# One load for the values of a turn, the output products ahead of them, and closing products in four column groups: an attention decode step on one core

## The chip, the core and the metric

The kernel runs on one core of a Trainium2 chip. Time is device time in microseconds (us) of one launch, and the smaller is the better. Before the change three runs gave 220.52, 220.58 and 221.18 us; the median is 220.58 us.

The engines named here are TensorE (PE in the rows; its weight loads are PEld), VectorE (DVE), ScalarE (ACT), GpSimd (POOL) and SyncE (SP, which here only waits and asks for transfers). Sixteen DMA engines carry the transfers; all of this kernel's transfers stand in one queue that SP fills.

## The reference: what is computed

One decode step for a batch of two tokens, in float32. Two branches are mixed by a gate.

```python
g = sigmoid((x * gate_w).sum(-1))                  # x: 2 x 512
q = (x @ wq)                                       # 32 heads of 128
k, v = the last 4096 rows of the caches            # 8 key heads, each shared by 4 query heads
p = softmax(q k^T / sqrt(128));  o = p v
a = o @ wo                                         # wo: 4096 x 512
b = mish(x @ w1 + b1) @ w2                         # 512 -> 1792 -> 512
out = g * a + (1 - g) * b                          # 2 x 512
```

Per key head, K and V of both batches are 4 MB each, wq's and wo's share 1 MB each. Everything that is read is read once, 91.26 MB in all.

## The kernel before, in words

The work goes in eight turns, one for each key head, in a hardware loop on each engine (`Fori(1, HKV + 1)`). SP's part is written out, without a loop. There is one buffer for K with the next turn's wq (`kslot`, 40 KB per partition) and one for V with w2's and wo's share (`vslot`). Semaphores tie the engines together; `ld_...` are counted up by transfers, 16 for each.

In a turn TensorE does the scores (L233), a small transpose for the maximum (L239), the sum of the exponentials (L240), the values (L244), the second product of the dense branch (L253), a selection of the attention output (L257) and the output products with wo (L260). Scores, values, w2 and wo products are 32 columns wide on the output side, so four of them stand in the four column groups of the array and run at the same time. A float32 matmul shows up as two instructions in the rows.

The dense branch and the output products lag by a turn: the `wst` and `hst` that L260 and L253 multiply in turn r were written by GpSimd at the end of turn r-1 (semaphore `hs`), and the wo and w2 that come into `vslot` beside V of turn r are those of turn r-1. They add into `acc`, in PSUM, over all turns. What is left after the eighth turn, wo of the last head, comes in three loads into `wol` and is multiplied by the closing products (L267), which add it up in `fin` with the folded `acc` (through `accs`, ScalarE's copy at L218).

VectorE in a turn makes the next turn's queries (L325, which end in `qz`), the maximum (L329), the transposed probabilities `pT` (L335), the dense branch's first product (L336, L292, L298), scales the attention output (L342, L344, giving `osel`), and copies the selected output into `wst2` (L347, semaphore `wst`).

SP's order for turn i (counted from 0): wait for `qz`, so that the scores are done with `kslot`; ask for K of turn i; wait for `sV`, which TensorE counts up after the first half of the values; ask for the first half of V (`va`); wait for `sP`, which it counts up at the end of the turn, after L260; ask for the second half of V with w2 and wo (`vb`). The last turn's K, V, w2 and wo come in smaller pieces, and the closing wo in three (`wo7a`, `wo7b`, `wo7c`). After that SP waits for `res` and stores the 4 KB result.

At the end, TensorE's closing products write two rows of 256 columns at a time: for u of 0 and 1 into column groups 0 and 1 or 2 and 3. ScalarE copies one half out (L220, `fs`), VectorE adds the other to it (L351).

Of the kernel before, what the change touches and what calls it, by code (L numbers as in the profile page):

```python
# [3 lines left out]
F32 = mybir.dt.float32  # L4
# [4 lines left out]
P = 128  # L9
B = 2  # L10
# [26 lines left out]
def decode_kernel(nc, xg, wq0, w1, kw, k7a, k7b, k7c, va, vb0, vb, v7b, v7c, w26, wo6, wo7a, wo7b, wo7c, out):  # L37
# [5 lines left out]
    def ps(name, n):  # L43
# [6 lines left out]
    vslot = sb("vslot", CHUNK + 2 * D + WQH + 2 * HKV)  # L50
    vs, w2s, wos = vslot[:, :CHUNK], vslot[:, CHUNK : CHUNK + 2 * D], vslot[:, CHUNK + 2 * D : CHUNK + 2 * D + WQH]
    b1 = vslot[:, CHUNK + 2 * D + WQH : CHUNK + 2 * D + WQH + FC]
# [41 lines left out]
    fs = sb("fs", 256, 64)  # L94
    res = sb("res", 256, 64)
# [10 lines left out]
    names = ("ld_x ld_q ld_k ld_kb ld_kc ld_v ld_vb ld_vc ld_w ld_h ld_o ld_w0 ld_w1 ld_w2 c_id c_m c_z c_xb c_eg c_g c_mg "  # L106
             "gx g0 g1 g2 g3 g4 g5 hs vx q8 rcp os1 os2 os3 qz mx sA sB bias ex pT sC osel sD sP sE sV wst pq mkr w1c w1p hx hq hd hr accs pe fs res st").split()
# [3 lines left out]
    SP.dma_start(vslot[:, CHUNK + 2 * D : CHUNK + 2 * D + WQH + FC], wq0).then_inc(sem["ld_q"], L)  # L111
# [4 lines left out]
    for i in range(HKV):  # L116
# [7 lines left out]
        if i:  # L124
            SP.wait_ge(sem["sV"], i)
        SP.dma_start(vs[:, : 2 * h], va[i]).then_inc(sem["ld_v"], L)
        if i:
            SP.wait_ge(sem["sP"], i)
        if i == 0:
            SP.dma_start(vs[:, 2 * h :], vb0).then_inc(sem["ld_vb"], L)  # L130
            SP.dma_start(w1s[:, : PAIRS * W1P], w1).then_inc(sem["ld_w"], L)
        elif i < PAIRS:
            SP.dma_start(vslot[:, 2 * h : CHUNK + 2 * D + WQH], vb[i - 1]).then_inc(sem["ld_vb"], L)
        else:
            SP.dma_start(vs[:, 2 * h : 3 * h], v7b).then_inc(sem["ld_vb"], L)
            SP.dma_start(vs[:, 3 * h :], v7c).then_inc(sem["ld_vc"], L)
            SP.dma_start(w2s, w26).then_inc(sem["ld_h"], L)  # L137
    SP.dma_start(wos, wo6).then_inc(sem["ld_o"], L)
# [69 lines left out]
    for n in ("ld_kb", "ld_kc", "ld_vc", "ld_o", "ld_h"):  # L208
        A.sem_inc(sem[n], AHEAD)
# [9 lines left out]
    A.wait_ge(sem["pe"], 1)  # L219
    A.copy(fs, fin[64:, :256]).then_inc(sem["fs"], 1)  # L220


    key_rhs = same[:, :16].rearrange("p (b n h) -> p b n h", b=B, n=NH)[:, :, 0, :]
    with T.Fori(1, HKV + 1, 1) as r:
# [16 lines left out]
        T.wait_ge(sem["ld_v"], loads)  # L241
        for c in range(NC):
# [162 lines left out]
```

## Time and profile before

| what | value |
|---|---|
| three runs, median | 220.58 us |
| profiled execution, its own time | 220.1 us |
| its span, first to last instruction of the program | 218.8 us |
| moved | 91.26 MB, 417 GB/s over the span |
| mean granted TensorE clock | 0.797 of full |
| TensorE busy / VectorE busy | 118.8 us / 126.2 us |

The profiled execution's time is 1.3 us above its span (220.1 - 218.8) and 0.5 us under the median of the three runs. Its rows read like this: a start and a duration in us from the span's start, engine, line of the kernel, operation, what it writes and reads, how many instructions the row stands for, and in brackets how long the engine was idle before it and what ended that.

### The profile page before, as it was taken

The numbers are of one execution on the slowest core, as the hardware profiler recorded it, in microseconds if no ns is written. First come the engines' busy times: TensorE is split into PE (matmuls) and PEld (weight loads), VectorE is DVE, ScalarE is ACT, GpSimd is POOL, SyncE is SP. The second block draws the span as 40 slices with busy tenths as digits, with TensorE's granted clock in tenths as the row PEclk, the third lists the DMA queues.
The fourth block names the chain that finished last, engine by engine and source line by source line (L and its number), as shares of the span: only waits on it lengthen the run. The fifth ranks groups of instructions, "written<-read, shape, count | busy, mean of one in ns | idle before, by whom it ended". The sixth has DMA issues, their size and how long they took to land.

```text
span 218.8 us, 1985 instructions
## 1 busy us (share of the span) xinstructions
PE 118.8 (54%) x668; PEld 31.1 (14%) x668; DVE 126.2 (58%) x268; ACT 10.3 (5%) x28; POOL 26.2 (12%) x118
## 2 busy tenths in 40 slices
PE   0006386058463477807547195924648175984775
PEld 0002021012110112202111022101112022120211
DVE  2897913919743468507673177714693075967850
ACT  2000010000100001000100001000100001000101
POOL 8200000220021000310012000210002100050030
PEclk9999958757969675875988757695996958599599
DMA  8898999989999999989999899999999899999993
GB/s 310 367 479 371 453 446 407 479 377 429 451 434 442 401 437 455 464 374 452 435 407 479 377 429 446 439 442 401 437 455 464 374 446 440 392 412 442 412 410 118
DMA packets 4926, 91.29 MB, mean 417 GB/s; under 512 B 552, under 2 KB 572, under 8 KB 1084
## 3 DMA queue, kind: packets, MB, share of 16 engines
q1 hardware_dynamic: 4924, 91.26, 97.8%
q8 instruction: 1, 0.02, 0.0%
q14 instruction: 1, 0.01, 0.0%
HBM read 91.26 MB, written 0.00 MB: 417 GB/s over the span
## 4 chain that ended last, share of the span: by engine, by line
DMA 73%; PE 15%; DVE 8%; SPq 2%; issue 1%; DVEq 0%
DMA vslot<-in_vb 51%; DMA w1s<-in_w 15%; PE o L244 9%; DMA wol<-in_wo7a 8%; PE acc L260 4%; DVE osc L344 3%; PE small L257 1%; DVE osc L342 1%; DVE junk L292 1%; DVE hxt L298 1%; PE fin L267 1%; SPq L113 0%; DVE w1c L336 0%; DVE xs L300 0%; SPq L137 0%
## 5 line engine op out<-in xcount | busy, mean ns | idle before, releaser
L233 PE MATMUL sc<-kslot,zeros 128*32 128x512 f32 x256 | 42.7, 823 | 51.5 <-DMA kslot<-in_kw 50.2
L325 DVE CUSTOM_DVE_ANT_0 junk<-kslot,xs 128x512 f32<-128x512 f32 x64 | 39.8, 686 | 37.4 <-DMA kslot<-in_kw 36.4
L244 PE MATMUL o<-vslot,pT 128*32 128x512 f32 x256 | 48.2, 897 | 12.8 <-DMA vslot<-in_vb 10.1
L233 PEld LDWEIGHTS sc<-kslot,zeros 128*32 128x32 f32 x256 | 10.7, 145 | 83.2 <-issue 80.4
L187 POOL TENSOR_TENSOR hb<-hxt,zeros 128x4 f32<-128x4 f32 x8 | 1.7, 216 | 147.0 <-DVE hxt L298 147.0
L292 DVE TENSOR_TENSOR junk<-w1c,xs 128x2048 f32<-128x2048 f32 x8 | 18.3, 2293 | 0.3
L298 DVE TENSOR_REDUCE hxt<-junk 128x4 f32<-128x2048 f32 x8 | 18.3, 2286 | 0.3
L244 PEld LDWEIGHTS o<-vslot,pT 128*32 128x32 f32 x256 | 9.2, 147 | 42.4 <-issue 19.1
L342 DVE TENSOR_SCALAR osc<-o,mkr 128x128 f32<-128x128 f32 x8 | 2.8, 351 | 15.1 <-PE o L244 15.1
L214 ACT ACTIVATE prob<-sc,bias 128x512 f32<-128x512 f32 x8 | 5.5, 687 | 118.7 <-DVE bias L333 118.7
L257 PE MATMUL small<-same,osc 128*128 128x8 f32 x16 | 3.3, 280 | 12.7 <-DVE osc L344 12.7
L240 PE MATMUL small<-lsum,same 128*128 128x1 f32 x16 | 4.1, 324 | 10.5 <-ACT prob L214 10.5
L260 PE MATMUL acc<-vslot,zeros 128*32 128x512 f32 x64 | 9.4, 662 | 0.6 <-DMA vslot<-in_wo 0.6
L335 DVE STREAM_TRANSPOSE pT<-prob 128x512 f32<-128x512 f32 x8 | 5.7, 712 | 6.8 <-ACT prob L214 6.8
L336 DVE COPY w1c<-w1s 128x1024 f32 x8 | 5.2, 656 | 7.5 <-DMA w1s<-in_w 7.5
L344 DVE SCALAR_TENSOR_TENSOR osc<-o,mkr,osc 128x128 f32<-128x128 f32 x24 | 8.4, 351 | 0.9
L253 PE MATMUL acc<-vslot,zeros 128*32 128x512 f32 x32 | 8.6, 616 | 0.3 <-DMA vslot<-in_w 0.3
L329 DVE TENSOR_REDUCE mx<-sc 128x1 f32<-128x512 f32 x8 | 5.5, 691 | 5.6 <-PE sc L233 5.6
L239 PE MATMUL mb<-ident,mx 128*128 128x128 f32 x8 | 2.6, 322 | 9.1 <-DVE mx L329 9.1
L257 PEld LDWEIGHTS small<-same,osc 128*128 128x128 f32 x16 | 2.6, 203 | 20.2 <-DVE osc L344 20.2
L325 DVE DVE_READ_ACCUMULATOR2_ANT q<- 128x1 f32 x64 | 5.2, 81 | 0.0
L240 PEld LDWEIGHTS small<-lsum,same 128*128 128x128 f32 x16 | 3.4, 265 | 12.0 <-ACT prob L214 12.0
(63 smaller groups left out, 64.8 us busy)
## 6 DMA issues: line engine op xcount, KB each, us to landing
kslot<-in_kw SPq DMA_DIRECT2D x7, 5120.0 KB, 19.3
vslot<-in_vb SPq DMA_DIRECT2D x6, 3584.0 KB, 18.9
vslot<-in_va SPq DMA_DIRECT2D x8, 2048.0 KB, 19.9
w1s<-in_w SPq DMA_DIRECT2D x1, 3584.0 KB, 32.7
vslot<-in_vb SPq DMA_DIRECT2D x1, 2048.0 KB, 24.6
kslot<-in_k7a SPq DMA_DIRECT2D x1, 2048.0 KB, 11.1
vslot<-in_wq SPq DMA_DIRECT2D x1, 1031.0 KB, 5.2
kslot<-in_k7b SPq DMA_DIRECT2D x1, 1024.0 KB, 13.2
```

The lines of the kernel that those rows point to most:

```text
L214: A.activation(prob, sc, AF.Exp, bias=bias, scale=SCALE, accum_out=lsum).then_inc(sem["ex"], 1)
L233: i = T.matmul(sc[Q * j : Q * j + Q, :], qz[:, m * Q : m * Q + Q], ks[:, (m * NJ + j) * 512 : (m * NJ + j + 1) * 512], start=(m == 0), sto ...
L240: after(T.matmul(lp, same, lsum, start=True, stop=True), "ex").then_inc(sem["sC"], 1)
L244: i = T.matmul(o[Q * j : Q * j + Q, :], pT[:, c * Q : c * Q + Q], vs[:, c * 512 : c * 512 + 512], start=(c < NJ), stop=(c >= NC - NJ))
L253: i = T.matmul(acc[Q * j : Q * j + Q, :], hst[:, j * Q : j * Q + Q], w2s[:, j * D : j * D + D], start=False, stop=False, skip_group_check= ...
L257: after(T.matmul(ol, osel, key_rhs, start=True, stop=True), "osel").then_inc(sem["sE"], 1)
L260: i = T.matmul(acc[Q * j : Q * j + Q, :], wst[:, j * Q : j * Q + Q], wos[:, j * D : j * D + D], start=False, stop=False, skip_group_check= ...
L292: return V.tensor_tensor(out.rearrange("p (b c d) -> p b c d", b=B, c=n), lhs.rearrange("p (c d) -> p c d", c=n)[:, None, :, :].to_broadca ...
L298: return V.tensor_reduce(out, junk[:, : n * D].rearrange("p (c d) -> p c d", d=D), axis=AX.X, op=ALU.add)
L325: i = V.tensor_tensor_reduce(out=junk[:, (h * B + b) * D : (h * B + b) * D + D], in0=wqs[:, h * D : h * D + D], in1=xb[b], op0=ALU.mult, o ...
L335: after(V.transpose(pT, prob), "ex").then_inc(sem["pT"], 1)
L344: after(V.scalar_tensor_tensor(osc[:, m * DH : m * DH + DH], o[:, m * DH : m * DH + DH], mkr[:, m : m + 1], osc[:, m * DH - DH : m * DH], ...
```

## The change

Three things are changed.

First, V of a turn comes in one load. `vslot` now begins with 64 bytes that hold b1 in the first turn, then wo, V and w2 in this order. Turns 1 to 6 have one load for the whole row (`vw`, 44 KB per partition), turn 0 one for V, and in turn 7 wo's share comes with the first half of V (`v7a`). The semaphore `sV` is gone; SP asks for the whole of V after `sP`.

Second, TensorE's order in a turn: the four wo products stand ahead of the values, the two w2 products behind the values as before, and `sP` is now counted up behind w2, ahead of the selection product. The loop's first instruction is put at an address that is a multiple of 256 (`T.addr_align`).

Third, the closing products. Each of the five operands is multiplied by four matmuls of 128 columns, one in each column group; the folded `acc` comes first; VectorE copies the sum out at once (128 x 128), and ScalarE's copy and the addition are gone. The output is stored from eight rows of 512 bytes.

```diff
-        if i:
-            SP.wait_ge(sem["sV"], i)
-        SP.dma_start(vs[:, : 2 * h], va[i]).then_inc(sem["ld_v"], L)
-        if i:
-            SP.wait_ge(sem["sP"], i)
         if i == 0:
-            SP.dma_start(vs[:, 2 * h :], vb0).then_inc(sem["ld_vb"], L)
+            SP.dma_start(vs, v0).then_inc(sem["ld_v"], L)
             SP.dma_start(w1s[:, : PAIRS * W1P], w1).then_inc(sem["ld_w"], L)
-        elif i < PAIRS:
-            SP.dma_start(vslot[:, 2 * h : CHUNK + 2 * D + WQH], vb[i - 1]).then_inc(sem["ld_vb"], L)
+            continue
+        SP.wait_ge(sem["sP"], i)
+        if i < PAIRS:
+            SP.dma_start(row, vw[i - 1]).then_inc(sem["ld_v"], L)
         else:
+            SP.dma_start(row[:, : WQH + 2 * h], v7a).then_inc(sem["ld_v"], L)
             SP.dma_start(vs[:, 2 * h : 3 * h], v7b).then_inc(sem["ld_vb"], L)
             SP.dma_start(vs[:, 3 * h :], v7c).then_inc(sem["ld_vc"], L)
             SP.dma_start(w2s, w26).then_inc(sem["ld_h"], L)
-    SP.dma_start(wos, wo6).then_inc(sem["ld_o"], L)
...
+    T.addr_align(256, offset=0, max_nops=0)
...
         T.wait_ge(sem["ld_v"], loads)
+        for j in range(REP):
+            i = T.matmul(acc[Q * j : Q * j + Q, :], wst[:, j * Q : j * Q + Q], wos[:, j * D : j * D + D],
+                         start=False, stop=False, skip_group_check=True)
+            if j == 0:
+                after(i, "hs")
         for c in range(NC):
...
-            if c == NC // 2 - 1:
-                i.then_inc(sem["sV"], 1)
         i.then_inc(sem["sD"], 1)
         T.wait_ge(sem["ld_h"], loads)
         for j in range(2):
             i = T.matmul(acc[Q * j : Q * j + Q, :], hst[:, j * Q : j * Q + Q], w2s[:, j * D : j * D + D],
                          start=False, stop=False, skip_group_check=True)
-            if j == 0:
-                after(i, "hs")
+        i.then_inc(sem["sP"], 1)
         after(T.matmul(ol, osel, key_rhs, start=True, stop=True), "osel").then_inc(sem["sE"], 1)
-        T.wait_ge(sem["ld_o"], loads)
-        for j in range(REP):
-            i = T.matmul(acc[Q * j : Q * j + Q, :], wst[:, j * Q : j * Q + Q], wos[:, j * D : j * D + D],
-                         start=False, stop=False, skip_group_check=True)
-        i.then_inc(sem["sP"], 1)
-
-    def last(s, lhs, rhs, wait=None, **kw):
-        for u in range(2):
-            a = Q * (2 * s + u)
-            i = T.matmul(fin[a : a + Q, :256], lhs, rhs[:, u * 256 : u * 256 + 256], skip_group_check=True, **kw)
-            if wait is not None and u == 0:
+    def last(lhs, rhs, wait, **kw):
+        for u in range(NJ):
+            i = T.matmul(fin[Q * u : Q * u + Q, :P], lhs, rhs[:, u * P : u * P + P], skip_group_check=True, **kw)
+            if u == 0:
                 i.wait_op(*wait, "sem-ge")
         return i
+    last(fold, accs, (sem["accs"], 1), start=True, stop=False)
     T.wait_ge(sem["wst"], HKV)
-    last(0, *wo(0), (sem["ld_w0"], L), start=True, stop=False)
-    last(1, *wo(1), start=True, stop=False)
-    last(0, fold, accs, (sem["accs"], 1), start=False, stop=False)
-    last(1, *wo(2), (sem["ld_w1"], L), start=False, stop=True).then_inc(sem["pe"], 1)
-    last(0, *wo(3), (sem["ld_w2"], L), start=False, stop=True).then_inc(sem["pe"], 1)
+    for j, (n, value) in enumerate((("ld_w0", L), ("wst", HKV), ("ld_w1", L), ("ld_w2", L))):
+        i = last(wst2[:, j * Q : j * Q + Q], wol[:, j * D : j * D + D], (sem[n], value), start=False, stop=(j == REP - 1))
+    i.then_inc(sem["pe"], 1)
...
-    A.wait_ge(sem["pe"], 1)
-    A.copy(fs, fin[64:, :256]).then_inc(sem["fs"], 1)
...
-    V.wait_ge(sem["fs"], 1)
-    at(V.tensor_tensor(res, fin[:64, :256], fs, op=ALU.add), "pe", 2).then_inc(sem["res"], 1)
+    at(V.tensor_copy(res, fin[:, :P]), "pe", 1).then_inc(sem["res"], 1)
```

TensorE's program from the values of a turn to the end, before. `o` takes the values, `acc` the products with wo and w2, `small` the selection, `fin` the closing products; in brackets what an instruction waits for.

```order
L244 MATMUL o<-vslot,pT 32x512 [waits ld_v,pT]
L244 MATMUL o<-vslot,pT 32x512 x7
L244 MATMUL o<-vslot,pT 32x512 [waits ld_vb]
L253 MATMUL acc<-vslot,zeros 32x512 [waits ld_h,hs]
L257 MATMUL small<-same,osc 128x8 [waits osel]
L260 MATMUL acc<-vslot,zeros 32x512 [waits ld_o]
L267 MATMUL fin<-wol,wst 32x256 [waits wst,ld_w0]
L267 MATMUL fin<-accs,fold 32x256 [waits accs]
L267 MATMUL fin<-wol,wst 32x256 [waits ld_w2]
```

The same stretch of the changed program, whose lines are numbered by its own file.

```order
L238 MATMUL acc<-vslot,zeros 32x512 [waits ld_v,hs]
L238 MATMUL acc<-vslot,zeros 32x512 x3
L244 MATMUL o<-vslot,pT 32x512 [waits pT]
L244 MATMUL o<-vslot,pT 32x512 x7
L251 MATMUL acc<-vslot,zeros 32x512 [waits ld_h]
L254 MATMUL small<-same,osc 128x8 [waits osel]
L258 MATMUL fin<-accs,fold 32x128 [waits accs]
L258 MATMUL fin<-wol,wst 32x128 [waits wst,ld_w0]
L258 MATMUL fin<-wol,wst 32x128 [waits ld_w2]
```

The four wo products (L260 before, L238 now) moved from behind the selection to ahead of the values, and the whole group now waits for the one load `ld_v`; the folded `acc` moved to the front of the closing products.

SP's requests in the last turn and at the end, before:

```order
L123 DMA kslot<-in_k7c 128x2048
L126 DMA vslot<-in_va 128x4096 [waits sV]
L135 DMA vslot<-in_v7b 128x2048 [waits sP]
L136 DMA vslot<-in_v7c 128x2048
L137 DMA vslot<-in_w 128x1024
L138 DMA vslot<-in_wo 128x2048
L140 DMA wol<-in_wo7a 128x1024
L355 DMA out<-res 4x256 [waits res]
```

And now:

```order
L122 DMA kslot<-in_k7c 128x2048
L131 DMA vslot<-in_v7a 128x6144 [waits sP]
L132 DMA vslot<-in_v7b 128x2048
L133 DMA vslot<-in_v7c 128x2048
L134 DMA vslot<-in_w 128x1024
L136 DMA wol<-in_wo7a 128x1024
L341 DMA out<-res 4x2x128 [waits res]
```

wo's 1 MB moved from behind w2 into the load of V's first half, ahead of the rest of V, and that load now waits for `sP`. SP has 28 requests in all where it had 36; eight loads are gone, by joining two into one in each turn.

More of the change, by code (lines that the diff above doesn't have):

```diff
@@ L34, with decode_kernel @@
 NP = PAIRS - 1
-def decode_kernel(nc, xg, wq0, w1, kw, k7a, k7b, k7c, va, vb0, vb, v7b, v7c, w26, wo6, wo7a, wo7b, wo7c, out):
+def decode_kernel(nc, xg, wq0, w1, kw, k7a, k7b, k7c, v0, vw, v7a, v7b, v7c, w26, wo7a, wo7b, wo7c, out):
     T, V, A, G, SP = nc.tensor, nc.vector, nc.scalar, nc.gpsimd, nc.sync
@@ L49, in decode_kernel @@
     w1c = sb("w1c", W1P)
-    vslot = sb("vslot", CHUNK + 2 * D + WQH + 2 * HKV)
-    vs, w2s, wos = vslot[:, :CHUNK], vslot[:, CHUNK : CHUNK + 2 * D], vslot[:, CHUNK + 2 * D : CHUNK + 2 * D + WQH]
-    b1 = vslot[:, CHUNK + 2 * D + WQH : CHUNK + 2 * D + WQH + FC]
+    vslot = sb("vslot", Q // B + WQH + CHUNK + 2 * D)
+    b1, row = vslot[:, :FC], vslot[:, Q // B :]
+    wos, vs, w2s = row[:, :WQH], row[:, WQH : WQH + CHUNK], row[:, WQH + CHUNK :]
     wol = sb("wol", REP * D)
@@ L93, in decode_kernel @@
     accs = sb("accs", D)
-    fs = sb("fs", 256, 64)
-    res = sb("res", 256, 64)
+    res = sb("res", P)
     acc = ps("acc", D)
@@ L104, in decode_kernel @@
     ol = small[:, 8:16]
-    names = ("ld_x ld_q ld_k ld_kb ld_kc ld_v ld_vb ld_vc ld_w ld_h ld_o ld_w0 ld_w1 ld_w2 c_id c_m c_z c_xb c_eg c_g c_mg "
-             "gx g0 g1 g2 g3 g4 g5 hs vx q8 rcp os1 os2 os3 qz mx sA sB bias ex pT sC osel sD sP sE sV wst pq mkr w1c w1p hx hq hd hr accs pe fs res st").split()
+    names = ("ld_x ld_q ld_k ld_kb ld_kc ld_v ld_vb ld_vc ld_w ld_h ld_w0 ld_w1 ld_w2 c_id c_m c_z c_xb c_eg c_g c_mg "
+             "gx g0 g1 g2 g3 g4 g5 hs vx q8 rcp os1 os2 os3 qz mx sA sB bias ex pT sC osel sD sP sE wst pq mkr w1c w1p hx hq hd hr accs pe res st").split()
     sem = {n: nc.alloc_semaphore(n) for n in names}
-    SP.dma_start(vslot[:, CHUNK + 2 * D : CHUNK + 2 * D + WQH + FC], wq0).then_inc(sem["ld_q"], L)
+    SP.dma_start(vslot[:, : Q // B + WQH], wq0).then_inc(sem["ld_q"], L)
     SP.wait_ge(sem["c_xb"], 2)
@@ L205, in decode_kernel @@
                         omg[:, None, :].to_broadcast([P, 2, B]), op=ALU.mult).then_inc(sem["hs"], 1)
-    for n in ("ld_kb", "ld_kc", "ld_vc", "ld_o", "ld_h"):
+    for n in ("ld_kb", "ld_kc", "ld_vb", "ld_vc", "ld_h"):
         A.sem_inc(sem[n], AHEAD)
@@ L349, in decode_kernel @@
     V.addr_align(128, offset=0, max_nops=0)
-    V.wait_ge(sem["fs"], 1)
-    at(V.tensor_tensor(res, fin[:64, :256], fs, op=ALU.add), "pe", 2).then_inc(sem["res"], 1)
+    at(V.tensor_copy(res, fin[:, :P]), "pe", 1).then_inc(sem["res"], 1)
     SP.wait_ge(sem["res"], 1)
-    SP.dma_start(out, res[:: Q // B, :]).then_inc(sem["st"], L)
+    SP.dma_start(out.rearrange("b u x -> u b x"), res[:: Q // B, :]).then_inc(sem["st"], L)
     SP.wait_ge(sem["hs"], HKV + 1)
@@ L388 @@
         "k7a": k[PAIRS, :, : 2 * h], "k7b": k[PAIRS, :, 2 * h : 3 * h], "k7c": k[PAIRS, :, 3 * h :],
[L389 to L391 removed]
+        "v0": v[0],
+        "vw": np.concatenate([wo[: NP], v[1:PAIRS], w2[:NP]], axis=2),
+        "v7a": np.concatenate([wo[NP], v[PAIRS, :, : 2 * h]], axis=1),
         "v7b": v[PAIRS, :, 2 * h : 3 * h], "v7c": v[PAIRS, :, 3 * h :],
[L393 removed]
+        "w26": w2[NP],
         "wo7a": wo[PAIRS, :, : 2 * D], "wo7b": wo[PAIRS, :, 2 * D : 3 * D], "wo7c": wo[PAIRS, :, 3 * D :],
```

14 lines of the change are left out of this document (4 added, 10 removed).

## The prediction

> **What bounds the kernel now.** I read the page first: how much of the span the transfers fill, and who stands on the chain that ended last.
>
> ```profile
> span 218.8 us, 1985 instructions
> DMA  8898999989999999989999899999999899999993
> q1 hardware_dynamic: 4924, 91.26, 97.8%
> DMA 73%; PE 15%; DVE 8%; SPq 2%; issue 1%; DVEq 0%
> ```
>
> The one queue is busy for 97.8% of the span; only the first and the last slice show a gap. So a wait on an engine costs time only where it leaves the queue empty or where it stands behind the last transfer. The chain in order of time shows both places: V of turns 5 and 6 landing, then the last turn's requests, and what follows the last piece of wo. The first row of the second fence is from the timeline of TensorE: it started the moment the last piece of wo had landed.
>
> ```profile
> 144.57 19.49 DMA vslot<-in_vb
> 170.66 18.92 DMA vslot<-in_vb
> 197.50 16.89 DMA wol<-in_wo7a
> 215.78 0.65 PE fin L267 x4
> 216.46 0.42 DVE res L351
> ```
>
> ```profile
> 215.78 0.14 PEld L267 LDWEIGHTS fin<-wol,wst 128*32 128x32 f32 x4 [0.52 <-DMA wol<-in_wo7c]
> 216.90 0.57 SPq L355 DMA_DIRECT2D out<-res  x1
> ```
>
> The last load lands at about 215.75; call this time E. What is behind it is 0.65 us of closing products, 0.42 us of VectorE, and the store. Last I read SP's own waits, since the change alters when SP may ask.
>
> ```profile
> SPq L133 <- PE acc L260: 52.9, 6, 13.2
> SPq L126 <- PE o L244: 33.7, 7, 5.7
> SPq L357 <- DMA out<-res: 1.1, 1, 1.1
> ```
>
> SP waits for TensorE for long, but asks so early that the queue always holds work: in the chain, V was asked for 19 us before it landed.
>
> **The change part by part.** *Eight loads fewer.* V of turn 5 landed at 164.06 (144.57 + 19.49), V of turn 6 at 189.58 (170.66 + 18.92). Between them lie 25.52 us for K, half of V, and the rest with weights: 5120 + 2048 + 3584 = 10752 KB in 3 loads. From 189.58 to E lie 26.17 us, for 4096 KB of K, 4096 of V, 512 of w2, 1024 and 1024 of wo: again 10752 KB, in 11 loads. The 8 extra loads cost 0.65 us, 0.08 each. The change joins two loads into one in each of the eight turns, so it saves at most 8 x 0.08 = 0.65 us by this row. Part of the 0.65 is the end itself, where no load follows and the sixteen engines finish unevenly; if it were all of it, the saving would be 0. I take 0.5, nearer to the row.
>
> *When V is asked for.* Before, the first half of V was asked for halfway through the values, the rest at the turn's end. Now SP waits for one group: wo (2 steps), values (8) and w2 (2), where I call a step four matmul instructions side by side in the four column groups. These rows give the price of a step and of a burst of 8; the first two are of the view by stretches of time, and the number ahead of the last two in each is the granted TensorE clock.
>
> ```profile
> 194.50:199.50 5.00, 3.72 (x35) 0.99 (x35) 4.65 (x17) 0.00 (x0) 1.91 (x4) 1.00 1.06 444
> 204.00:209.30 5.30, 4.81 (x24) 1.13 (x24) 5.16 (x5) 0.00 (x0) 0.19 (x1) 0.55 1.00 416
> 206.17 0.22 PEld L244 LDWEIGHTS o<-vslot,pT 128*32 128x32 f32 x4 [0.63 <-issue]
> 207.02 0.23 PEld L244 LDWEIGHTS o<-vslot,pT 128*32 128x32 f32 x4 [0.63 <-DMA vslot<-in_v7b]
> 195.46 0.13 PEld L233 LDWEIGHTS sc<-kslot,zeros 128*32 128x32 f32 x4 [0.30 <-issue]
> 195.89 0.13 PEld L233 LDWEIGHTS sc<-kslot,zeros 128*32 128x32 f32 x4 [0.30 <-issue]
> 18.24 4.99 PE L233 MATMUL sc<-kslot,zeros 128*32 128x512 f32 x32 [18.24 <-DMA kslot<-in_kw]
> 28.99 6.43 PE L244 MATMUL o<-vslot,pT 128*32 128x512 f32 x32 [0.16 <-DVE pT L335]
> 74.19 6.02 PE L233 MATMUL sc<-kslot,zeros 128*32 128x512 f32 x32 [5.53 <-DMA kslot<-in_kw]
> 99.73 5.21 PE L233 MATMUL sc<-kslot,zeros 128*32 128x512 f32 x32 [6.34 <-DMA kslot<-in_kw]
> 176.32 6.16 PE L233 MATMUL sc<-kslot,zeros 128*32 128x512 f32 x32 [5.72 <-DMA kslot<-in_kw]
> 199.49 1.07 PE L233 MATMUL sc<-kslot,zeros 128*32 128x512 f32 x8 [1.28 <-DMA kslot<-in_k7c]
> ```
>
> A step takes 0.85 us (206.17 to 207.02) while the granted clock is at about half (0.55 in that stretch), and 0.43 (195.46 to 195.89) at full (1.00). Bursts of 8 steps that begin after a pause took 4.99 to 6.43, 5.8 in the mean of these five, according to when the clock rose. The new group has 12 steps: 4 more at 0.43 make 6.7 to 8.15. It begins when V has landed. K of the next turn is then in the queue and lands 12.26 us later (164.06 to 176.32), in the last turn, where K has no wq beside it, 9.91 us later (189.58 to 199.49). A request takes up to 1.7 us to bring its first bytes: the 4 KB store had landed 0.57 + 1.1 us after it was asked for at 216.90. So V must be asked for by 10.5 us after the landing in most turns and by 8.2 in the last. Both hold, the second with 0.05 to 1.5 us to spare. I cost the later request at 0, bounds 0 and 0.7 (a group that takes 0.7 us longer than the longest above); it has lost its cover of before.
>
> What is queued behind SP's new wait is the wait for `qz` and the next K, wanted only after that turn's scores. Behind the values on VectorE stand L342 to L348 and then the next turn's queries, which wait for K anyway.
>
> [...]
>
> *The last turn's end.* This is where the change adds work on the path. Before, wo's 1 MB came behind w2; now it comes ahead of V's second half, and the values of the last turn are that much later.
>
> ```profile
> 196.55 0.43 SPq L137 DMA_DIRECT2D vslot<-in_w  x1
> 197.02 0.43 SPq L138 DMA_DIRECT2D vslot<-in_wo  x1
> vslot<-in_wo SPq DMA_DIRECT2D x1, 1024.0 KB, 16.1
> vslot<-in_w SPq DMA_DIRECT2D x1, 512.0 KB, 14.1
> ```
>
> ```profile
> 204.49 5.95 PE L244 MATMUL o<-vslot,pT 128*32 128x512 f32 x32 [0.90 <-DMA vslot<-in_va]
> 209.38 0.16 PEld L244 LDWEIGHTS o<-vslot,pT 128*32 128x32 f32 x8 [1.27 <-DMA vslot<-in_v7c]
> 210.59 0.35 DVE L342 TENSOR_SCALAR osc<-o,mkr 128x128 f32<-128x128 f32 x1 [1.32 <-PE o L244]
> 212.57 0.17 DVE L347 COPY wst<-small 128x8 f32<-128x8 f32 x1 [0.48 <-PE small L257]
> 215.79 0.37 ACT L220 COPY fs<-fin 64x256 f32<-64x256 f32 x1 [0.93 <-PE fin L267]
> 216.46 0.42 DVE L351 TENSOR_TENSOR res<-fin,fs 64x256 f32<-64x256 f32 x1 [3.63 <-PE fin L267]
> ```
>
> w2 landed at 210.65 (196.55 + 14.1), wo at 213.12: wo's load takes 2.47. V's first half, at 204.46, was 11.3 ahead of E, and its last quarter, at 209.36, 6.4. With wo in front they are 8.8 and 3.9 ahead. So the last burst begins at E - 8.8: 10 steps until the values are done, 5.85 to 7.3 (8 steps and 2 x 0.43), but not before the last quarter and 1.23 us more (209.36 to 210.59). VectorE then starts between E - 2.7 and E - 1.5, and its chain to the copied `wst2` takes 2.15 us (210.59 to 212.57 + 0.17). Four closing products follow, of two steps each with 128 columns instead of 512, so a quarter of 0.43 per step: 0.86 for the four, and the 0.22 that the last product of before showed beyond its two half-length steps (0.65 - 0.43). They end between E + 0.55 and E + 1.75; with the mean burst (10 steps in 6.65) VectorE starts at E - 2.1 and they end at E + 0.95. Before it was E + 0.68 (216.43). Cost: 0.3 us, bounds -0.15 and +1.1. The fold ahead of them waits for `accs`, which comes 0.6 us behind w2's two steps, inside VectorE's 2.15; the same cover hides the loop's exit.
>
> *The copy.* 0.42 us for 64 x 256 of two operands becomes a copy of 128 x 128 of one. Between L347's 0.17 (128 x 8) and L342's 0.35 (128 x 128 from PSUM) I take 0.3: a gain of 0.1, bounds 0.07 and 0.25. ScalarE's copy ended at 216.16, before `fin` was done: 0. The store is the same 4 KB: 0, by the 1.67 us it took, 0.1 either way. The aligned loop: TensorE's pause at re-entry is 0.30 (the weight load at 195.46), and in all turns but the last K is awaited there: 0, or 0.3 either way.
>
> Sum: -0.5 + 0 + 0.3 - 0.1 = -0.3 us on the profiled execution's 220.1, which is 0.48 under the median. On the median it gives 220.58 - 0.3 = 220.3. The best ends give -0.65 - 0.15 - 0.25, about -1.0; the worst 0 + 0.7 + 1.1 - 0.07, +1.7.
>
> **Rivals.** *The clock rises early in the last burst.* Then the closing products are hidden up to the last piece of wo, E + 0.55, and the saving of loads is all kept: -0.5 - 0.15 - 0.1, 219.8, or 219.6 with the row's full 0.65. For it: bursts of 4.99 and 5.21. Against: three of the five took 6 us or more.
>
> *The queue runs dry in the last turn*, the slower side. V's pieces are asked for only behind the 12 steps; past 8.2 us after the landing each microsecond is one of an empty queue. If the clock stayed at half for the whole group, 12 x 0.85 = 10.2: 2.0 us, 222.3. For it: 8 steps in 6.43 us from 28.99 is nearly all at half clock. Against: no burst here stayed at half for longer, and 8.15 still fits.
>
> [...]
>
> [...]
>
> [...]
>
> **How the numbers follow.** Forecast (the two ends cancel) 0.42, early clock 0.30, dry queue 0.16, the 64 bytes 0.12. 0.3%, 0.66 us, is about what a measurement of this kernel tells from no change: faster means below 219.92, slower above 221.24. The early clock gives 0.25 of faster, the forecast 0.04 of either sign through its burst; the dry queue 0.13 of slower, the 64 bytes 0.03 together with a late clock. Faster 0.29, same 0.51, slower 0.20. The range runs from 219.5 (early clock with the row's saving) to 221.5 (a late clock with little saved, or a queue dry for about a microsecond); the forecast's own is 219.8 to 221.0.
>
> **What would show it.** Right: the time between two landings of V falls from 25.52 by 0.06; SP asks for V 6.7 to 8.2 us after the landing, and the queue has no gap before the last V; E comes 0.5 earlier, and the products end more than 0.55 behind E when the last burst was at half clock for long. Wrong: landings of V as far apart as before or farther (the joining saves nothing, or the offset costs), a gap in the transfers near 199, or a product that ends within 0.5 of E at any clock.

## The result: 1.0% slower, outside the range

The changed kernel takes 223.64 us in the median of 19 executions (220.84 to 225.41); the kernel before, in the same series, 220.49 (220.11 to 221.55, 19). The ratio is 1.0099, 95% interval 1.0073 to 1.0126. (Executions over 1.5% above the fastest of their kernel, six of the changed kernel's 19 here, are not counted in a ratio; the medians have all of them.) By the medians of all executions it is 1.4% (223.64 / 220.49). The prediction was 220.3, range 219.5 to 221.5; its own worst ends, +1.7, would have given 222.3.

Not only the middle moved: the executions of the changed kernel lie 4.6 us apart, those of the kernel before 1.4. The change also made the time differ more from one execution to the next.

### The profile page after: what moved, and what is told of

Read it like the earlier page. It is cut to its first block, busy times and chain, and to the rows that moved or that the text cites. A ratio compares the mean times of both kernels' runs of the same rounds, so it can differ in the third digit from the quotient of the medians.

```text
span 222.3 us, 2008 instructions
## 1 busy us (share of the span) xinstructions
PE 113.7 (51%) x688; PEld 35.4 (16%) x688; DVE 126.0 (57%) x268; ACT 10.0 (4%) x27; POOL 26.1 (12%) x118
## 3 DMA queue, kind: packets, MB, share of 16 engines
q1 hardware_dynamic: 3776, 91.26, 96.5%
## 4 chain that ended last, share of the span: by engine, by line
DMA 69%; PE 27%; DVE 1%; issue 1%; SPq 0%; DVEq 0%
DMA vslot<-in_vw 53%; PE o L244 17%; DMA vslot<-in_v 12%; PE acc L238 7%; DMA vslot<-in_v7a 5%; PE acc L251 3%; PE fin L258 1%; DVE osc L331 0%; SPq L112 0%; DVE xs L287 0%; SPq L119 0%; PE small L254 0%; DVE osc L329 0%; DVE res L337 0%; DVEq L328 0%
## 5 line engine op out<-in xcount | busy, mean ns | idle before, releaser
L244 PE MATMUL o<-vslot,pT 128*32 128x512 f32 x256 | 39.3, 765 | 0.0
L238 PE MATMUL acc<-vslot,zeros 128*32 128x512 f32 x64 | 15.4, 1050 | 31.0 <-DMA vslot<-in_vw 29.3
L228 PEld LDWEIGHTS sc<-kslot,zeros 128*32 128x32 f32 x256 | 11.5, 146 | 66.5 <-issue 66.5
L244 PEld LDWEIGHTS o<-vslot,pT 128*32 128x32 f32 x256 | 12.2, 147 | 31.6 <-issue 31.3
L235 PE MATMUL small<-lsum,same 128*128 128x1 f32 x16 | 3.9, 311 | 10.5 <-ACT prob L210 10.5
L251 PE MATMUL acc<-vslot,zeros 128*32 128x512 f32 x32 | 8.3, 592 | 0.0
L238 PEld LDWEIGHTS acc<-vslot,zeros 128*32 128x32 f32 x64 | 1.8, 136 | 31.4 <-issue 31.4
L195 POOL TENSOR_TENSOR mn<-mn,mr 128x4 f32<-128x4 f32 x8 | 1.6, 198 | 38.2 <-DVE mr L335 38.2
```

The lines of the kernel that those rows point to most:

```text
L228: i = T.matmul(sc[Q * j : Q * j + Q, :], qz[:, m * Q : m * Q + Q], ks[:, (m * NJ + j) * 512 : (m * NJ + j + 1) * 512], start=(m == 0), sto ...
L238: i = T.matmul(acc[Q * j : Q * j + Q, :], wst[:, j * Q : j * Q + Q], wos[:, j * D : j * D + D], start=False, stop=False, skip_group_check= ...
L244: i = T.matmul(o[Q * j : Q * j + Q, :], pT[:, c * Q : c * Q + Q], vs[:, c * 512 : c * 512 + 512], start=(c < NJ), stop=(c >= NC - NJ))
L251: i = T.matmul(acc[Q * j : Q * j + Q, :], hst[:, j * Q : j * Q + Q], w2s[:, j * D : j * D + D], start=False, stop=False, skip_group_check= ...
```

## The profile after

The profiled execution took 223.64 us, its span 222.3, 3.5 more than before. From its page:

```profile
span 222.3 us, 2008 instructions
...
q1 hardware_dynamic: 3776, 91.26, 96.5%
```

The queue's share fell from 97.8% to 96.5% of a longer span: the same bytes, with more time in which an engine of the sixteen moves none. The chain of waits shows it turn by turn. It now runs through V in every turn, as a row of V's load from its request to its landing, and then the group of products that SP waits for:

```profile
36.67 26.76 DMA vslot<-in_vw
...
63.56 1.94 PE acc L238 x8
65.50 4.39 PE o L244 x32
69.89 0.87 PE acc L251 x4
...
70.77 18.11 DMA vslot<-in_vw
...
97.14 17.71 DMA vslot<-in_vw
...
122.08 18.23 DMA vslot<-in_vw
...
148.46 17.94 DMA vslot<-in_vw
...
173.46 18.41 DMA vslot<-in_vw
...
193.94 5.02 PE o L244 x32
...
199.84 10.06 DMA vslot<-in_v7a
...
218.96 1.11 PE fin L258 x32
...
220.09 0.29 DVE res L337
```

Start plus duration gives V's landings: 63.43, 88.88, 114.85, 140.31, 166.40, 191.87. They are 25.45, 25.97, 25.46, 26.09 and 25.47 apart; before it was 25.53. Set beside them how long after the landing ahead of it SP asked (start of the row less that landing): 7.3, 8.3, 7.2, 8.1, 7.1. Where the group took 7.1 to 7.3, the turn is 0.07 shorter than before, as the joined loads should make it; where it took over 8, half a microsecond is lost. Whether it takes 7 or 8 goes with the clock that TensorE was granted from the landing to the request: 0.74 to 0.77 in the mean of the three groups of 7.1 to 7.3 us, 0.65 to 0.68 in the three of 8.0 to 8.3 (the last turn's, 7.97, among them). The values (L244) took 4.39 us in the first of the two turns shown and 5.02 in the other. These are the stretches of those two rows; the number ahead of the last two, the granted clock, was 0.80 in the first and 0.70 in the other.

```profile
65.50:69.89 4.39, 4.39 (x34) 1.26 (x28) 0.00 (x0) 0.00 (x0) 0.75 (x4) 0.80 1.04 448
193.94:198.96 5.02, 5.02 (x34) 1.35 (x28) 0.00 (x0) 0.21 (x1) 0.99 (x6) 0.70 0.97 410
```

The busy share of the DMA engines over the last turn, by stretches (the last two numbers are that share and GB/s):

```profile
199.00:202.00 3.00, 1.97 (x14) 0.64 (x14) 2.15 (x7) 0.00 (x0) 0.51 (x2) 1.00 0.69 218
202.00:205.00 3.00, 2.86 (x28) 0.78 (x20) 3.00 (x11) 0.00 (x0) 1.41 (x3) 1.00 0.93 393
```

Around the request at 199.84 the queue holds nothing for some engines: counted from the single packets, where sixteen are under way in a steady stretch, there were between one and nine in the 1.6 us behind it. V lands 18.03 after V of the turn before (17.17 where it is asked for early, below).

The first 10 us hold a loss of their own. These are the transfers' summary and SP's requests in that stretch, of the changed kernel:

```profile
q8 instruction: 1, 0.02, 1.2%
...
vslot<-in_wq SPq DMA_DIRECT2D x1, 1032.0 KB, 6.9
```

```profile
2.79 1.78 SPq L124 DMA_DIRECT2D vslot<-in_v  x1
```

and the same request of the kernel before, whose first 10 us have no second queue:

```profile
2.80 0.43 SPq L126 DMA_DIRECT2D vslot<-in_va  x1
```

Its load of wq, in the transfers' summary:

```profile
vslot<-in_wq SPq DMA_DIRECT2D x1, 1031.0 KB, 5.2
```

A second queue appears: one load of 16 KB of instructions. It starts at 2.33 us and takes 1.87 us. Of the sixteen landings of wq one then stands apart: fifteen come by 5.88 us and the last at 7.61, so one DMA engine is late. wq lands after 6.9 us, where it took 5.2; SP's request for V needs 1.78 us, where it needed 0.43. V of turn 1 lands at 63.43; before, by its chain of waits, at 61.93:

```profile
46.24 15.69 DMA vslot<-in_vb
```

The last row for the sum is the last load's, asked for at 202.95, so that E, its landing, is 218.75 (215.75 before):

```profile
wol<-in_wo7c SPq DMA_DIRECT2D x1, 256.0 KB, 15.8
```

So the 3.5 us are: 1.50 until V of turn 1 (63.43 against 61.93); 0.79 from there to V of turn 6 (128.44 against 127.65: two late turns, less 0.07 in the three others); 0.71 from there to E (26.88 against 26.17); 0.64 from E to the end of the products (1.32 against 0.68); -0.13 in the copy (0.29 against 0.42). Sum 3.51.

## The experiments

All times in one list; two single executions more of the kernel without alignment are in the text. Each ratio is to executions of the kernel before in the same series; their medians lie between 220.20 and 220.49. "Align" is the loop at an address that is a multiple of 256; "V" says in how many loads a turn's V comes and when the last turn's is asked for.

```
what is run                          median (range, executions)    ratio to before, 95%
changed kernel                       223.64 (220.84-225.41, 19)    1.0099  1.0073-1.0126
the same again, second series        222.80 (221.66-224.42, 4)     1.0131  1.0074-1.0188
V in two loads, asked early          221.40 (220.91-221.68, 4)     1.0049  1.0033-1.0066
before + closing products            220.62 (219.82-220.95, 8)     1.0010  0.9991-1.0029
changed + 5 warming products         221.01 (220.01-221.87, 5)     1.0028  1.0004-1.0052
changed, no align                    220.98 (219.46-224.95, 10)    1.0043  1.0018-1.0068
before + align                       220.87 (220.57-221.50, 10)    1.0026  1.0011-1.0042
no align + 5 warming products        219.65 (219.27-221.04, 12)    0.9982  0.9964-1.0001
no align, V in two loads             220.94 (219.94-222.07, 10)    1.0027  1.0010-1.0044
no align, request 2.6 us later       235.96 (235.65-236.27, 2)     1.0710  1.0683-1.0738
no align + 6 warming products        220.66 (219.75-221.28, 12)    1.0021  1.0007-1.0034
no align, last V asked early         220.67 (219.90-222.03, 12)    1.0012  0.9994-1.0029
no align, 5 warming, last V early    219.61 (219.38-220.37, 12)    0.9972  0.9961-0.9983
```

**Again.** The changed kernel, unaltered, in a second series.

> The changed kernel once more, for a second profile of it. Late request (SP asks for V 7.1 to 8.3 us behind its landing, and the DMA engine that is furthest ahead has run out by then): landings of V are 25.46 us apart where the request came within 7.4 us and 25.9 to 26.1 where it came after 8 us or more, and the last turn loses another 0.7. Uneven start (one of the sixteen engines comes 1.6 us late out of the first loads and never catches up): if the changed start causes it, the spread between the first and the last engine is again above 1.5 us at the landing of the first V; if it is chance, it is about 0.5 here and the time is 1.2 us lower for it.

222.80, and the same marks: the instruction load at the start (2.40 us), a late turn (25.75 between two landings of V), and V of the last turn 17.9 after the one before. It is no accident of one execution.

**V in two loads, asked early.** The change, but wo and the first half of V are asked for after half of the values, the rest at the turn's end.

```diff
+        SP.wait_ge(sem["sV"], i)
+        SP.dma_start(row[:, : WQH + 2 * h], vwa[i - 1] if i < PAIRS else v7a).then_inc(sem["ld_v"], L)
         SP.wait_ge(sem["sP"], i)
-            SP.dma_start(row, vw[i - 1]).then_inc(sem["ld_v"], L)
+            SP.dma_start(row[:, WQH + 2 * h :], vwb[i - 1]).then_inc(sem["ld_vb"], L)
```

> V in two loads again (wo with the first half, asked for after the first half of the values; second half with w2, asked for at the group's end), all else as changed: wo ahead, four column groups at the end. Late request: the queue never runs dry, landings of V 25.53 apart, 221 or below, spread 0.1% as before. Uneven start by the single load of the first V: gone too, since that load is in two again, so r1 must tell the two apart. Closing products as the main cost: the last turn's order is kept, so 222.5 to 223.5 stays.

221.40, where 221 or below was expected: asking early gives back 1.4 us of the 2.6 by which the changed kernel is slower in this series (222.80 against 220.20), not all. Its chain goes through K instead of V for most of its length, so V's request no longer sets the pace. What is left stands at the start (K of turn 0 lands at 19.41, 18.10 before) and at the end (the products end 1.2 behind E, 0.68 before).

**The closing products alone.** The kernel before with the third part of the change only: four column groups, the folded `acc` first, one copy.

> The kernel before with the new closing products and the one copy alone. By the working of the prediction: the products end 0.2 earlier behind the last load (0.45 for 0.65) and the copy takes 0.3 for 0.42, so 0.3 us off: 220.2. If issuing sixteen instructions for eight costs what the shorter columns save: 220.5.

220.62, ratio 1.001, with 1 inside its interval (0.9991 to 1.0029), where 220.2 was expected. The rows of its end, from the timeline:

```profile
215.66 1.06 PE L263 MATMUL fin<-wol,wst 128*32 128x128 f32 x32
216.79 0.29 DVE L342 COPY res<-fin 128x128 f32<-128x128 f32 x1 [3.15 <-PE fin L263]
```

The last load landed at 216.23, the products ended at 216.72, 0.49 behind it (0.68 before), and the copy takes 0.29 where it took 0.42. So behind E this part saves its 0.3 us. The median does not show it. E itself lay 0.5 later in this profile than in that of before, and so did already the landing of K of turn 0 (18.64 against 18.11), ahead of everything that this version changes; the spans of the kernel before alone go from 218.6 to 220.0 in this series. It is not what makes the changed kernel slow.

**Five warming products.** The changed kernel with five products of 128 x 512 more in each turn, four behind the scores and one ahead of the wait for V. They write `fin`, which nobody reads before the closing products start it anew; nothing is left out.

```diff
+        for _ in range(4):
+            T.matmul(fin, same, xs[:, :D], start=True, stop=True)
         after(T.transpose(mb[:, :P], mx.to_broadcast([P, P]), ident), "mx").then_inc(sem["sB"], 1)
         after(T.matmul(lp, same, lsum, start=True, stop=True), "ex").then_inc(sem["sC"], 1)
+        T.matmul(fin, same, xs[:, :D], start=True, stop=True)
```

Ahead of the loop TensorE also waits for the two operands that these products read (`c_m` and `c_xb`); every version below with extra products has these two waits.

> The changed kernel with five extra products of 128 x 512 in each turn, four behind the scores and one ahead of the wait for V, into a bank that nothing reads before the end, so that TensorE's clock stays at full when V lands. Nothing is left out. Late request: the group of twelve steps then takes 5.2 to 5.5 us, SP asks 5.5 us behind the landing, no queue runs dry, and the time falls to 219.5 to 220.5, with the last burst short as well. Uneven start alone: no change of more than 0.7 (the last burst).

More work, and faster than the change: 221.01 against 222.80 in the same series (ratios 1.0028 and 1.0131), though not the 219.5 to 220.5 that was expected. The chain of waits:

```profile
88.76 1.06 PE acc L243 x8
89.83 3.43 PE o L249 x32
93.26 0.86 PE acc L256 x4
94.14 19.94 DMA vslot<-in_vw
...
119.59 19.95 DMA vslot<-in_vw
```

The group takes 1.06 + 3.43 + 0.86 us; the 3.43 of the values are 0.43 for each of 8 steps, the time of a step at a granted clock of 1.00 in the kernel before (195.46 to 195.89). Over the whole profiled execution the granted clock was 0.876 in the mean, where it was 0.774 in the second series' profile of the changed kernel. So V is asked for 5.5 us after its landing, and lands every 25.46. This is the price of the late request by itself, taken away by making the group shorter rather than by asking at another place. Left over is the start: this kernel has the instruction load at 2.31 us too. And in two of its five executions the time is 2.0 and 2.4 us above the span instead of 1.3, of which more below.

**The alignment, taken from the change and put into the kernel before.** One line each.

```diff
-    T.addr_align(256, offset=0, max_nops=0)
```

> The changed kernel without the aligned loop, nothing else. Code fetch (the aligned loop makes TensorE fetch 16 KB of instructions 2.3 us into the run, through one of the sixteen DMA engines; that engine starts 2 us late and never catches up): no fetch ahead of 200 us, spread at the landing of the first K 0.45 to 0.95 instead of 1.65, 1.0 to 1.2 us off for the start alone, and since the furthest engine is then not so far ahead, landings of V stay 25.46 apart at 8 us too; 220.8 to 221.6. Late request without it (the start is chance): 222.5 to 223.

> The kernel before with the aligned loop alone. Code fetch: the spread at the first K is 1.6 to 1.9, the fetch stands near 2.3 us, and the last load lands 1.2 us later, all of it kept to the end: 221.4. If the alignment does nothing that is seen: 220.2.

On the kernel before, the line alone costs 0.26% (0.11 to 0.42), 0.57 us, half of the 1.2 that was expected. In its profile's first 10 us, the second queue and the request for V:

```profile
q8 instruction: 1, 0.02, 0.6%
```

```profile
2.79 0.83 SPq L126 DMA_DIRECT2D vslot<-in_va  x1
```

Without the line the changed kernel has no such load there, wq lands after 5.1 us and SP asks for V in 0.42; the 16 KB come at 216.89, behind the landing of the last load (215.08). The kernel before has its own at 215.49. How a delay of 2 us on one of sixteen engines lasts for 216 us is in the landings of single engines (my reading of the trace's landings; the spread is the time from the first engine's landing of a load to the last's):

```
spread of a load over the engines, us     wq     K of turn 0   last load   E
before                                    0.70   0.45          0.51        215.74
before + align                            1.76   1.59          1.56        216.83
changed kernel                            2.64   1.74          0.75        218.72
changed, no align (fastest profile)       0.62   0.43          0.55        215.08
```

In the kernel before with the line one landing of wq stands apart again (6.74, the next 5.80), and from K of turn 0 to the last load the spread stays between 1.56 and 1.61 us: this is what an engine that starts late and does not catch up would leave, with a queue that is never empty. At E this is 1.1 us between the two profiles; between the median spans it is 0.65 (219.55 against 218.9). (In the changed kernel the queue runs down to a single packet in the last turn, at 200.7 us, and the spread goes from 2.20 us at V of turn 6 to 0.78 at the last turn's first load of V, at its own price.)

Without the line the changed kernel's best profile (219.46) is all that the prediction's forecast described:

```profile
35.52 26.14 DMA vslot<-in_vw
...
171.37 17.57 DMA vslot<-in_vw
...
196.04 10.20 DMA vslot<-in_v7a
```

V lands every 25.456 us ((188.94 - 61.66) / 5), 0.074 less than before, the last V 17.30 after the one ahead of it, E is 0.66 earlier (0.12 of it stands already at K of turn 0, 17.99 against 18.11). But its executions go from 219.46 to 224.95, so two more executions of it were profiled, and both cures tried together.

**Two more profiles of the kernel without the alignment.**

> The changed kernel without the aligned loop, one more profile: its ten runs went from 219.46 to 224.95 and the one profile is of the fastest. Late request: in a slower run the landings of V are more than 25.5 apart in the turns whose group ran longest at half clock, and the last turn is 0.5 to 1.5 longer than the 17.3 us (V of turn 6 to the first half of the last V) of the fast one.

> The same kernel a third time, for the same question: more than 25.5 us between landings of V, or a last turn above 17.3 us, in a run above 220; no such turn in a run below.

223.95 and 221.33. The slow one's chain in the last turns:

```profile
172.57 17.61 DMA vslot<-in_vw
...
197.49 12.69 DMA vslot<-in_v7a
```

In the last turn V is asked for 7.31 us after the landing (197.49 - 190.18) and lands 20.0 after it: 2.8 us lost, more than the request was late. In the other profile 7.52 cost 0.95, in the fast profile 7.10 cost 0.13. Between the spans of the slow one and of the fast profile lie 4.5 us: 2.7 in the last turn, 1.1 in two turns between them, whose requests came 8.3 after the landing, and 0.65 behind E.

**Warming products without the alignment; V in two loads without it.**

> The changed kernel without the aligned loop and with the five extra products that keep TensorE's clock up. Code fetch and late request together: both losses gone, what is left is the saving of eight loads (0.5) and the shorter closing products and copy; 219.4 to 219.8, faster than before by 0.2 to 0.4%. If a third cost is left in the last turn, 220.2 or above.

> V in two loads, wo ahead of the values, without the aligned loop. Code fetch: 1.2 off the 221.4 of the same kernel with it. No saving of loads (one more is saved than before: none but wo's in the last turn), so 220.2 to 220.6, the difference to before being the last burst, which wo's load ahead of V still delays.

With the group short and no instruction load at the start: 219.65, ratio 0.9982 (0.9964 to 1.0001), as expected. V in two loads stays at 220.94, where 220.2 to 220.6 was expected. It gives up the saving of the joined loads in the turns between, and its profile shows no late turn; its time there is 2.28 us above its span of 218.67, where its nine other executions have 1.3 to 1.4; its instruction load stands behind the last instruction, of which more below. Why its median span of 219.55 is 0.65 above that of the kernel before isn't settled.

**Later still.** Without alignment, three products between w2 and `sP`, so that V is asked for 2.6 to 2.8 us later in each turn.

```diff
+        for _ in range(3):
+            i = T.matmul(fin, same, xs[:, :D], start=True, stop=True)
         i.then_inc(sem["sP"], 1)
```

> The changed kernel without the aligned loop, with three extra products of 128 x 512 behind w2 and ahead of the count that lets SP ask for V: about 2.6 us later each turn at full clock (nothing is left out). Late request: SP asks 9.7 to 11 us behind the landing of V, the engine furthest ahead has run out by 9.6 (next K 12.1, less the spread of 0.45, less 0.5 from the last packet to the count, less 1.6 from request to first packet), so landings of V move from 25.46 to 25.6 to 27 apart and the last turn loses 2.5 to 3.5: 226 to 230. If a late request cost nothing, 2.6 us at the very end at most: 222 to 223.

235.96, 15 us more than without them, where 226 to 230 was expected. V's loads from its chain:

```profile
71.31 16.53 DMA vslot<-in_vw
...
98.03 18.54 DMA vslot<-in_vw
...
127.75 15.91 DMA vslot<-in_vw
```

V landed at 87.84, 116.57 and 143.66. The request 10.2 us after the first of these (98.03) made a turn of 28.73, 3.3 too long; the one 11.2 us after the second (127.75) one of 27.09, 1.6 too long. So lateness alone does not give the loss: the later of the two requests cost half as much. The spread over the engines was 2.90 us at the first of these two late landings and 0.72 at the second; that the loss hangs on how the engines come out of a restart fits this, and is not shown.

**A sixth warming product,** between the transpose and the sum of the exponentials.

> As the kernel without the aligned loop and with five extra products, and a sixth between the transpose and the sum of the exponentials, where TensorE idles for 1.3 us. Late request and cold clock: no turn's group starts at half clock any more (two of eight did with five), runs within 0.3% of each other, 219.3 to 219.6. If the slow runs have another cause, 219.65 with the same scatter to 221.

220.66, and by the median spans a loss of 1.0 us against five (219.3 for 218.3), where a gain was expected. The group took 5.5 us in turns 2 to 6, but 7.04 still in the last. The reason that the trace offers is in its profile in 200 to 202 us:

```profile
q8 instruction: 1, 0.02, 2.9%
```

With one product more an instruction load of 16 KB comes at 200.95 us, in the last turn; the profile with five has none. The spread over the engines goes from 0.54 to 1.75 us in the load that is under way, and E is 216.21 where it was 215.10. The same 16 KB at another time than the start, and again about 1.1 us. That V was asked for 7.04 us behind the landing does not explain it: with 7.10 and 7.13 us the last turn lost 0.13 in the profiles without such a load. It is one profile, and no run takes the load alone away.

**The last V asked for early.** Without alignment, and only in the last turn the request goes back to where half the values are done; first with nothing else, then with the five warming products.

```diff
+            SP.wait_ge(sem["sV"], i)
             SP.dma_start(row[:, : WQH + 2 * h], v7a).then_inc(sem["ld_v"], L)
+            SP.wait_ge(sem["sP"], i)
```

> The changed kernel without the aligned loop; only in the last turn SP asks for wo and the first half of V after half the values, as before the change, and for the last two quarters after the turn's products. The six turns between stay as in the change, with their request after the whole group. If the scatter of the kernel without alignment (219.46 to 223.95) comes from the restart of the queue in the last turn, this brings V of the last turn 17.2 us after V before it in every profile, and the times lie between 219.4 and 220.6 with no one above 221.3; median 220.0. If the six turns between do it (requests after 8.1 to 8.3 us, with 0.5 us lost in each such turn), the median stays near 220.9 and single times still go over 222.

> The same early request in the last turn together with the five extra products in each turn. Both places where the queue can run short are then covered: landings of V 25.46 apart in all middle turns, the last one 17.2 after V before it. Theory: 219.3 (219.0 to 219.7), ratio 0.995 to 0.998, with all executions within 0.8 of each other. If the early last request is worth nothing beside the warm products, it stays at 219.6 with the same scatter as that version alone (219.27 to 221.04).

The first: 220.67, with executions up to 222.03. That is neither alternative cleanly. None of the 12 executions lies above 222.1, where four of the twelve without the early request did, which fits the restart in the last turn as what made the slowest; but the median is 0.7 above what I expected if it made them all. Part of that lies outside the span: in five of the 12 the time is 1.6 to 2.3 us above it instead of 1.3. By the median spans the early request is worth 0.65 (219.05, and 219.7 in the ten executions without it). In its profile (222.03) the last V lands 17.17 after the one before, as it should, and the loss is in two late turns (8.3 us, 0.27 and 0.14 lost) and at the end, where the last burst started late and its ten steps up to the end of the values took 7.04 us, 0.70 each (0.43 at a granted clock of 1.00 and 0.85 at 0.55 in the kernel before):

```profile
207.93 1.86 PE acc L239 x8
209.79 5.18 PE o L245 x32
217.02 1.47 PE fin L261 x40
```

The products end at 218.49, 2.5 behind E (215.97).

The second: 219.61, ratio 0.9972 (0.9961 to 0.9983), the fastest version here and the only one whose interval lies under 1.

```profile
36.16 26.13 DMA vslot<-in_vw
...
67.80 19.94 DMA vslot<-in_vw
...
169.60 19.95 DMA vslot<-in_vw
```

V lands every 25.45 us ((189.55 - 62.29) / 5). Against the five warming products alone the early request is worth nothing within the span: the median span is 218.3 in both. The wider range of that version comes from outside it. In 4 of its 12 executions the time is 2.0 to 2.5 us above the span instead of 1.3; in none of the 12 here, nor in any of the kernel before.

**What a late request costs, over all these profiles.** For turns 2 to 6 of eleven profiles (of all runs but those with two loads and those with the order of before) I read from the single packets how long after SP's request the first engine was done with K and began with V, how long the slowest of the engines' first two V packets took (1.67 us when undisturbed), and what the time between V's landings lost against 25.455:

```
first V packet after request    turns   slowest early V packet, us   lost, us
3.0 and more                    32      1.67 to 2.07                 0.00 to 0.02
2.0 to 3.0                      16      1.68 to 3.28                 at most 0.02 in ten; 0.04 to 0.62 in six
under 1.7 (the engine waited)    7      2.1 to 3.3                   0.5 to 3.3
```

There is no cliff where the queue runs empty. Behind a request less than 3 us ahead of need the first packets of some engines already took up to twice their time (3.28 us for 1.67). In three of the six turns that lost time there (0.62, 0.27 and 0.04 us) sixteen packets were under way at every moment of the 6.5 us behind the request; in the other three it was one or two fewer for part of a microsecond. The spread over the engines stays wider afterwards (in the slow one of the two further profiles 0.50 us before its first late turn, 1.11 after it). Why the packets stretch is not shown by these traces.

## Why the prediction was wrong, by its own steps

*Eight loads fewer, -0.5 (0 to -0.65): right.* A turn is 0.07 shorter wherever the stream was not disturbed, and from K of turn 0 to E it takes 0.54 to 0.70 us less in the three profiles without a late turn in the middle (without alignment; the same with five products; with these and the last V early).

*V asked for later, 0 (0 to 0.7): this step failed.* Its first half nearly held: SP asked 7.06 to 8.26 us behind the landing in the changed kernel's profile, where 6.7 to 8.15 were worked out. The deadline was wrong: 10.5 us in most turns, 8.2 in the last. It set the landing of K less 1.7 us, the time from request to landing of the 4 KB store. Two things were left out. The first engine is done with K about 0.9 us before K's landing is counted (the spread of 0.45 and as much again from the last packet to the count). And the lead that a request for a load of 44 KB rows needed was 3 us by the table above (at most 0.02 us lost in all 32 turns that had it), not the 1.7 that the store of 4 KB took, with no load left in the queue. 12.1 - 0.9 - 3.0 is 8.2, and without the alignment the loss does begin there: 8.17 lost at most 0.04, 8.30 to 8.34 between 0 and 0.62. In the last turn, with 9.9 to K and rows of 24 KB, 5.5 lost nothing and 7.1 lost 0.13; nothing between was measured. The group's own range reaches past both. In the changed kernel this is 0.52 + 0.63 in two turns and 0.86 in the last, 2.0 us where 0 stood; with the alignment's wider spread the first engine is done earlier still (8.04 lost 0.29 in the second series). The upper bound was also of the wrong form: it let a request ahead of the deadline cost nothing and one microsecond behind it cost one. A request 7.3 us behind the landing in the last turn (deadline 8.2) lost 2.8 us, and one at 10.2 in another turn (deadline 10.5) 3.3. Two of the prediction's own signs of being wrong came: landings of V farther apart than before, and a gap in the transfers near 199.

*The last turn's end, +0.3 (-0.15 to +1.1): right in mechanism and within its bounds.* The products end at E + 1.32 in the changed kernel (0.64 later than before), at E + 0.8 in the fastest profile without the alignment. The middle of that sum has a slip: a VectorE start at E - 2.1 with 2.15, 0.86 and 0.22 behind it ends at E + 1.13, not E + 0.95, so the term should have read 0.45. One profile, with the last V asked for early, had E + 2.5, over the bound of 1.75: its burst started 0.8 us behind V's landing and took 7.0.

*The copy, -0.1: right,* 0.29 for an estimate of 0.3.

*The aligned loop, 0 or 0.3 either way: this step failed too.* The prediction asked what the line does to TensorE's pause at the loop's start. What the runs show is another thing: without the line a 16 KB load of instructions stands in the last 5 us of the program (215.49 in the kernel before), with it 2.3 us from the start, ahead of data whose delay was still there at E. It cost 0.57 us in the median of the kernel before, 1.1 us in its profile, 1.5 until V of turn 1 in the changed kernel's. The row to see it in was there before, and I passed over it as too small; this is the queue of instruction loads on that kernel's page:

```profile
q8 instruction: 1, 0.02, 0.0%
```

The load is one packet of 16384 bytes in the traces of both kernels, and the cost is that of the data of one late DMA engine. Whether the engine whose instructions these are itself waited was not measured.

*The rivals.* The dry queue in the last turn had the right direction and stood at 0.16, at 222.3; it missed that the turns between are affected at the same lateness. Its case against, that 8.15 still fits, was the wrong deadline. The early clock, 219.8, describes the version with warming products well (219.65), only that the clock had to be brought about: 0.867 in the mean of its profiled execution, 0.797 without those products. The 64 bytes, by which V's row now starts into its buffer, had a chance of 0.12 for what they might cost. No run shows such a cost: in the median of the changed kernel's trace V's packets of 45056 bytes take 1.665 us and K's of 40960 bytes, which start at the beginning of their buffer, 1.514, 27.1 bytes per ns for both; V's landings are 25.45 apart where nothing else disturbs them.

The parts do not add up: the alignment alone costs 0.26%, the change without it 0.43%, both together 0.99% in one set and 1.31% in another. The wider spread takes time from the lead of the late request. That this is the reason is argued from the two mechanisms; no run separates it.

**Open:** why early packets stretch; and part of the scatter without the alignment. The last turn's restart made the slowest profile (2.7 of its 4.5 us) and the warming products remove nearly all of the rest, but whether the rest lies in the turns between or in the long last burst (7.04 us for ten steps) was seen in one profile only, which had both.

## What to carry to other kernels

In a kernel whose one queue is never empty, ask of every request how long before the first engine runs out it comes, not before the last landing, and allow what a load needs (here about 3 us for rows of 44 KB); where it depends on a granted clock that differs from turn to turn, count its longest time (8.3 us here, with 7.1 as the shortest). A line that moves code can move instruction loads (here one of 16 KB, from 215.49 us to 2.3 us): look for them in the list of queues, by time, and keep them out of the stretches in which every DMA engine is needed. Work that only keeps TensorE's clock up (0.867 for 0.797 here) can pay when a request hangs on it: five products more per turn were worth 0.6%.

## What the hardware showed that I had not expected

- A load of 16 KB of instructions 2.3 us from the start, while wq was being loaded, cost the kernel before 0.57 us in the median and 1.1 us at E in the profile: one engine of sixteen was late, and the spread was still 1.6 us at E, for 0.5 before.
- In three profiles such a load comes after the last instruction (at about 220.1, 220.6 and 220.8 us, for spans of 218.7, 219.3 and 219.5). In these the time is 2.0 to 2.4 us above the span; in the thirteen others it is 1.3 to 1.5.
- The first packets behind a late request took up to 2.9 us for 1.67 in a turn in which sixteen packets were under way all the time. The quickest first packet came 0.95 us after its request.
